# A Conformer block on one core: the passage from the convolution to the second feed-forward rearranged, and some of VectorE's work changed

## The chip, the core and the metric

The kernel runs on one core of a Trainium2 chip. The metric is the device time in microseconds of one execution. Lower is better. TensorE does matrix products into PSUM banks; VectorE (DVE), ScalarE (ACT) and GpSimd (POOL) do element-wise work; SyncE (SP) issues most DMAs. The kernel has eight PSUM banks of 128 x 512 float32: s0 to s3 and y0 to y3.

## What is computed

The input x has 2 sequences of 4000 tokens with 512 features. The reference, cut to what matters:

```python
h = _layernorm(x);  h = _silu(h @ w_ff1_a) @ w_ff1_b
x1 = x + 0.5 * h
h = _layernorm(x1); q, k, v = h @ w_q, h @ w_k, h @ w_v
p = _softmax(jnp.einsum('btd,bsd->bts', q, k) * scale)
x2 = x1 + jnp.einsum('bts,bsd->btd', p, v) @ w_o
h = _layernorm(x2) @ w_pw1
h = h[..., :D] * _sigmoid(h[..., D:])
dc = sum(pad(h)[:, i:i + T, :] * dw[i] for i in range(3))      # depthwise convolution over time
dc = (dc - mean) / sqrt(var + 1e-5)                            # per feature, over all tokens of both sequences
x3 = x2 + _silu(dc) @ w_pw2
h = _layernorm(x3); h = _silu(h @ w_ff2_a) @ w_ff2_b
return _layernorm(x3 + 0.5 * h)
```

The normalisation of `dc` runs over all tokens, so that nothing behind it can start before the depthwise convolution of the last token.

## The kernel before, in words

The 8000 tokens are cut into 16 chunks of 512 (`NCK`); the last chunk of each sequence has 416. A chunk has four tiles of 128 tokens, the features four blocks of 128 (`DC`, the index `cc` or `jj`). The stages follow each other: first feed-forward over all chunks; attention over all chunks `g`, 32 key tiles `kt` each; the convolution, whose chunk t runs beside attention of chunk t+1; the second feed-forward.

**The order of work.** The kernel's functions don't issue instructions. Each operation becomes a `Node` of a `Plan`, with reads, writes, an estimated duration and an engine that is fixed when it is written. `Plan.once` then goes through time and gives every engine, whenever it is free, the ready node that is due first; TensorE's blocks may overtake each other within 8 us, and other engines look ahead 16 us. `Plan.run` does six such passes, takes the shortest by its own costs and emits the instructions in that order. So the order of the program states the dependences, and the plan makes the queues. Since all instructions are emitted from one helper, the profile gives L93 for nearly every line; groups are told apart by tiles: `work` (LayerNorm and small tiles, normalised tokens, queries, z), `keys` (keys, feed-forward activations, the depthwise result dcv), `sums` (forms for attention), `wff` (feed-forward weights, and during the convolution its buffers), `xt` (tokens), `s` and `y` (PSUM).

**Attention.** Exponentials go to bf16 tiles. `pair_sums` forms sums for a product scheme with seven products in place of eight and adds the row sums of each group of two tile pairs to the float32 tile `acc`, one addition per pair. When a chunk is finished, `split_sums` writes `acc` as two bf16 parts, `sums_by_query` transposes both by DMA and reduces them on VectorE (`TENSOR_REDUCE`), and a reciprocal gives `rl`, which `project` needs for the residual x2. `sums_direct` does the same by matmuls with a column of ones; before the change only the fallback program uses it.

**The convolution.** `conv_b` does the gate half of `pw1` and its Sigmoid (Tanh for earlier chunks), `conv_a` the other half and the product into `G`, with `halo_left` and `halo_right` copying edge columns between chunks. For chunks 0 to 12, and block 0 of chunk 13, `taps_beside` does the depthwise step beside attention: ScalarE multiplies by the first tap into a float32 `tmp`, two `scalar_tensor_tensor` on VectorE add the others, `bn_stats` takes statistics. The rest of chunk 13 and chunks 14 and 15 are done by `depthwise` on TensorE: three matmuls with diagonal matrices `dwd`, then statistics and a copy to `dcv`. `conv_part` gathers the statistics of the chunks so far, `conv_scale` and `conv_shift` give scale and shift, `swish` does the Silu.

**The passage.** After attention (`attention_end`), `program` projects chunk 15, normalises its tiles (`ln_tiles`), and fills TensorE with `pw1` of chunk 14 and depthwise of chunk 13. After chunk 15's transposes (`transpose_pair`), each block of chunk 15 gets `conv_b`, `conv_a`, and `finish`: depthwise of chunk 15 and of chunk 14, then the scale. `pw2_x` puts the tokens into PSUM with an identity, `pw2` adds Silu times w_pw2, `ln_tiles` normalises chunk 0's four tiles out of PSUM, two `transpose_pair` follow, and the first block of the second feed-forward starts. Chunk 1's four tiles are done the same way in between, and all eight are copied from PSUM to `XT`. `ff2(c)` is the second feed-forward of chunk c; its `hook(f)` places, at block f of 16, the Silus and `pw2` of chunks ahead and the LayerNorm of the next chunk.

Of the kernel before, what the change touches and what calls it, by code (L numbers as in the profile page):

```python
# [15 lines left out]
TILE = 128  # L16
# [88 lines left out]
class Node:  # L105

    __slots__ = ("e", "emit", "dur", "land", "preds", "succs", "left", "ready", "late", "at", "seq", "ev", "size", "turn")


class Plan:  # L110
# [62 lines left out]
    def new(self, e, dur, land, emit, reads, writes, dkeys=()):  # L173
        n = Node()
        n.e, n.dur, n.land, n.emit, n.preds, n.succs, n.seq, n.at = e, dur, land, emit, set(), [], len(self.nodes), len(self.pe)
        n.size, n.turn = 0, False
        self.nodes.append(n)
        n.preds |= self.link(n, reads, writes, dkeys)
        return n

    def op(self, e, fn, reads, writes, inc):
# [21 lines left out]
        self.block = [] if inc else [n]  # L203

# [31 lines left out]
    def run(self):  # L236
# [17 lines left out]
        for n in best[1]:  # L254
            for f in n.emit:
                f()

    def once(self):
# [7 lines left out]
        for n in self.nodes:  # L266
            n.left, n.ready = len(n.preds), 0.0
            if not n.left:
                wait[n.e].append(n)
# [4 lines left out]
        def choose(e):  # L274
# [17 lines left out]
            for n in can:  # L292
                end = now + max(n.dur, n.size / 260) + self.OVER[e]
# [7 lines left out]
        while len(order) < len(self.nodes):  # L301
# [3 lines left out]
            s, n = min([c for c in said.values() if c], key=lambda c: c[0])  # L305
            wait[n.e].remove(n)
            ask[n.e] = True
            free[n.e] = s + n.dur + self.OVER[n.e]
            order.append(n)
# [11 lines left out]
            for u in n.succs:  # L321
# [3 lines left out]
                if not u.left:  # L325
                    wait[u.e].append(u)
                    ask[u.e] = True
# [3 lines left out]
class Sync:  # L331
# [110 lines left out]

    def dma(self, e, dkey, *fns, reads=(), writes=()):
# [82 lines left out]
class Conformer:  # L526
# [9 lines left out]
    KEEP = 1  # L536

# [20 lines left out]
    def memory(self):  # L558
# [164 lines left out]
        self.asb = [W.view(8192 + k * 2048, CHUNK, F32) for k in range(3)]  # L723
        self.b_asb = [W.buf("asb", 8192 + k * 2048, 4 * CHUNK) for k in range(3)]
        self.tmp = W.view(12288, CHUNK, F32)
        self.b_tmp = W.buf("tmp", 12288, 4 * CHUNK)
# [7 lines left out]
        self.th = [W.view(24576 + s * 2048, CHUNK, F32) for s in range(2)]  # L734
        self.b_th = [W.buf("th", 24576 + s * 2048, 4 * CHUNK) for s in range(2)]
# [4 lines left out]
        self.b_z = [[C.buf("z", o + cc * 2 * CHUNK, 2 * CHUNK) for cc in range(DC)] for o in (oM, oQ0)]  # L740
        assert off[0] == 47104
# [230 lines left out]
    def away(self, eng, dst, src, b_ps, writes):  # L972

        if eng == "ACT":
            self.act(dst, src, AF.Copy, [b_ps], writes)
        else:
            self.S.op("DVE", lambda e: e.tensor_copy(dst, src), reads=[b_ps], writes=writes)
# [63 lines left out]
    def ln_stats(self, c, sl, ti, src=None):  # L1041
        x, b_x = self.tokens(c, ti, src)
        self.S.op("DVE", lambda e: e.bn_stats(self.st[sl][:, ti, 0:6], x), reads=[b_x], writes=[self.b_st[sl][ti]])
# [15 lines left out]
    def ln_norm(self, c, sl, ti, out, b_out, eng, src=None):  # L1059
        x, b_x = self.tokens(c, ti, src)  # L1060
        if eng == "DVE":
            self.S.op("DVE", lambda e: e.tensor_scalar(
                out, x, self.mv[sl][:, ti, 0:1], self.rs[sl][:, ti:ti + 1],
                ALU.subtract, ALU.mult),
                reads=[b_x, self.b_mv[sl][ti], self.b_rs[sl][ti]], writes=[b_out])
# [657 lines left out]
    def pair_sums(self, g, j, step):  # L1723
# [337 lines left out]
    def units_late(self, o, kt):  # L2061
# [5 lines left out]
        elif kt < 7:  # L2067
# [3 lines left out]
            if kt == 2:  # L2071
                self.split_sums(o)
                self.sums_by_query(o % TCB % 2, 5)
# [22 lines left out]
    def attention_end(self):  # L2096
# [102 lines left out]
    def split_sums(self, g):  # L2199
# [9 lines left out]
        for hi, lo, acc in parts:  # L2209
            S.op("DVE", lambda e: e.tensor_copy(hi, acc), reads=[self.b_acc[s]], writes=[self.b_hl[0]])  # L2210
# [57 lines left out]
    def conv_b(self, t, jj):  # L2268
# [6 lines left out]
        else:  # L2275
            self.act(self.th[k][:, 0:W], ps[:, 0:W], AF.Sigmoid, [b_ps], [self.b_th[k]])

    def conv_a(self, t, jj):
# [4 lines left out]
        out = self.G[gs][:, jj, 1:1 + W]  # L2283
        wr = [self.b_G[gs][jj], self.b_Gl[gs][jj], self.b_Gr[gs][jj]]
        if t == NCK - 2 and jj >= self.KEEP:

            asb, b_asb = self.asb[jj % 3], self.b_asb[jj % 3]
            self.act(asb, ps[:, 0:CHUNK], AF.Copy, [b_ps], [b_asb], scale=2.0)

            def gate(eng):  # L2290
                self.S.op(eng, lambda e: e.tensor_tensor(out=out, in0=asb, in1=th, op=ALU.mult),
                          reads=[b_asb, self.b_th[k]], writes=wr)
# [4 lines left out]
        elif t == NCK - 1:  # L2297
            self.S.op("DVE", lambda e: e.scalar_tensor_tensor(
                out=out, in0=ps[:, 0:W], scalar=2.0, in1=th, op0=ALU.mult, op1=ALU.mult),
                reads=[b_ps, self.b_th[k]], writes=wr)  # L2300
# [4 lines left out]
        if t < NCK - 1:  # L2305
            self.halo_left(t, jj)
# [18 lines left out]
    def taps_beside(self, t, cc):  # L2325
# [5 lines left out]
        tmp, b_tmp = self.tmp[:, 0:W], self.b_tmp  # L2331
        self.act(tmp, g[:, 0:W], AF.Identity, rd, [b_tmp], scale=w[0])
        S.op("DVE", lambda e: e.scalar_tensor_tensor(
            out=tmp, in0=g[:, 1:1 + W], scalar=w[1], in1=tmp, op0=ALU.mult, op1=ALU.add),
            reads=rd + [b_tmp], writes=[b_tmp])

        def rest():
            dst, b_dst = (self.stage[cc], self.b_stage[cc]) if t < self.NBESIDE else (self.dcv[t][cc], self.b_dcv[t][cc])
            dst = dst[:, 0:W]
            S.op("DVE", lambda e: e.scalar_tensor_tensor(  # L2340
                out=dst, in0=g[:, 2:2 + W], scalar=w[2], in1=tmp, op0=ALU.mult, op1=ALU.add),
                reads=rd + [b_tmp], writes=[b_dst])
            S.op("DVE", lambda e: e.bn_stats(self.bst[:, cc, t, :], dst),
                 reads=[b_dst], writes=[self.b_bst[cc]])
            if t == self.beside(cc) - 1:
# [7 lines left out]
    def beside(self, cc):  # L2353
        return self.NBESIDE + (cc < self.KEEP)

# [547 lines left out]
```

## Time and profile before

| | us |
|---|---|
| median of three runs | 1888.24 (1886.43 to 1888.3) |
| the profiled execution | 1886.77 |
| its span, first to last instruction | 1882.5 |
| busy: TensorE, VectorE, ScalarE, GpSimd | 1859.6, 1570.6, 1180.4, 129.9 |
| granted TensorE clock | 1.0 |

Times in the profile count from the start of the span. The first feed-forward ends near 378, attention near 1400, and the second feed-forward begins at 1439.79. A row of a timeline gives start, duration, engine, line, operation, the tiles written and read, sizes and types, how many instructions are merged, and in brackets the engine's idle time before it and what ended it. A row of a group gives the count, then busy time and the mean in ns of one, then the idle time ahead of it by releaser. A matmul's duration includes its latency, so consecutive ones overlap.

### The profile page before, as it was taken

To read this page: it belongs to the slowest core of one execution; us is meant where nothing else is said; L and a number is where in the kernel's file an instruction comes from. 1 tells how busy PE (TensorE), PEld (TensorE's weight loads), DVE (VectorE), ACT (ScalarE), POOL (GpSimd) and SP (SyncE) were. 2 spreads that over 40 slices of the span, in tenths; PEclk is the share of its full clock that TensorE was granted. 3 is DMA by queue.
4 is the path that set the end of the run, shared out by engine and by line. 5 is a ranking of instruction groups with operands and counts; after the bars stand their busy time and mean duration, and the time that the engine had idled before them with its cause. 6 is when DMAs were issued, how large, how long until landed. Compare 5 with 4: busy or idle time off the path is not lost.

```text
span 1882.5 us, 38836 instructions
## 1 busy us (share of the span) xinstructions
PE 1859.6 (99%) x15362; PEld 1442.7 (77%) x15362; DVE 1570.6 (83%) x3315; ACT 1180.4 (63%) x2061; POOL 129.9 (7%) x235
## 2 busy tenths in 40 slices
PE   9999999999999999999999999999998999999998
PEld 5888888866777777777677777777764888888886
DVE  7888888868879888888888788889877888888875
ACT  5777777644555665565446555655557777777773
POOL 1000000000000000000000000000011000000000
PEclk9999999999999999999999999999999999999999
DMA  7323344197555665448944443444365222212111
GB/s 190 102 78 91 81 113 107 61 263 214 173 143 141 172 168 162 108 131 176 239 143 131 126 123 105 124 141 121 109 209 169 77 57 69 78 46 60 50 43 33
DMA packets 327186, 232.01 MB, mean 123 GB/s; under 512 B 206355, under 2 KB 297814, under 8 KB 326742
## 3 DMA queue, kind: packets, MB, share of 16 engines
q1 hardware_dynamic: 326470, 229.20, 44.3%
q8 instruction: 123, 2.02, 0.4%
q14 instruction: 65, 0.53, 0.1%
q10 hardware_dynamic: 528, 0.26, 0.0%
HBM read 128.44 MB, written 55.79 MB: 98 GB/s over the span
## 4 chain that ended last, share of the span: by engine, by line
PE 93%; DVE 3%; ACT 1%; DMA 1%; issue 0%; POOL 0%; SPq 0%; DVEq 0%; ACTq 0%
PE y L93 47%; PE s L93 47%; DVE work L93 1%; ACT work L93 1%; DVE xt L93 1%; DMA work<-work 1%; DVE s L93 0%; DVE sums L93 0%; DVE wff L93 0%; ACT sums L93 0%; DMA vhd<-wff 0%; DMA xt<-in_x_dram 0%; DMA wff<-keysd 0%; ACT xt L93 0%; ACT keys L93 0%
## 5 line engine op out<-in xcount | busy, mean ns | idle before, releaser
L93 ACT ACTIVATE sums<-s 128x512 bf16<-128x512 f32 (+2 forms) x494 | 289.0, 586 | 262.4 <-PE s L93 261.6
L93 ACT ACTIVATE keys<-s 128x512 bf16<-128x512 f32 (+1 forms) x281 | 165.0, 589 | 186.8 <-PE s L93 170.3
L93 PE MATMUL y<-work,keys 128*128 128x256 bf16 x1920 | 244.7, 273 | 0.0
L93 DVE TENSOR_TENSOR sums<-sums 128x512 bf16<-128x512 bf16 (+3 forms) x528 | 192.4, 396 | 46.8 <-ACT sums L93 44.1
L93 PE MATMUL s<-work,keys 128*128 128x256 bf16 (+5 forms) x1456 | 224.9, 292 | 0.0
L93 DVE BATCH_NORM_STATS2 work<-xt 128x6 f32<-128x512 bf16 x311 | 205.3, 682 | 7.6 <-DMA xt<-in_x_dram 5.6
L93 PE MATMUL y<-wff,keys 128*128 128x256 bf16 (+3 forms) x1592 | 209.0, 276 | 0.1
L93 PEld LDWEIGHTS y<-work,keys 128*128 128x128 bf16 x1920 | 187.9, 98 | 25.2
L93 PE MATMUL y<-sums,keys 128*128 128x256 bf16 (+1 forms) x1440 | 200.9, 270 | 0.0
L93 PE MATMUL s<-sums 128*128 128x256 bf16 x1296 | 194.0, 273 | 0.0
L93 DVE TENSOR_TENSOR keys<-keys 128x1024 bf16<-128x1024 bf16 (+2 forms) x262 | 168.7, 662 | 19.9 <-ACT keys L93 14.0
L93 PE MATMUL y<-work,wff 128*128 128x256 bf16 (+2 forms) x1116 | 184.0, 292 | 0.0
L93 PEld LDWEIGHTS y<-wff,keys 128*128 128x128 bf16 (+1 forms) x1592 | 151.1, 98 | 32.6 <-issue 3.3
L93 ACT ACTIVATE work<-xt,work 128x512 bf16<-128x512 bf16 x204 | 161.8, 808 | 10.2 <-DVE work L93 10.1
L93 POOL TENSOR_TENSOR work<-work 128x4 f32<-128x4 f32 (+2 forms) x94 | 89.4, 952 | 1107.3 <-DVE work L93 1089.1
L93 PEld LDWEIGHTS y<-sums,keys 128*128 128x128 bf16 x1440 | 139.1, 98 | 24.1 <-issue 0.4
L93 PEld LDWEIGHTS s<-work,keys 128*128 128x128 bf16 (+1 forms) x1456 | 118.7, 97 | 49.7 <-issue 3.7
L93 DVE TENSOR_TENSOR work<-work,sums 128x512 f32<-128x512 f32 (+1 forms) x224 | 150.5, 672 | 2.5
L93 PE MATMUL s<-work,wff 128*128 128x512 bf16 (+4 forms) x660 | 139.9, 347 | 2.9 <-DVE work L93 1.5
L93 PE MATMUL y<-sums,xt 128*128 128x256 bf16 (+1 forms) x960 | 141.9, 270 | 0.5 <-DVE sums L93 0.5
L93 PEld LDWEIGHTS s<-sums 128*128 128x128 bf16 x1296 | 126.7, 98 | 20.0
L93 PE MATMUL s<-work 128*128 128x512 bf16 (+1 forms) x541 | 135.6, 380 | 1.9 <-DVE work L93 1.2
(133 smaller groups left out, 3136.1 us busy)
## 6 DMA issues: line engine op xcount, KB each, us to landing
xt<-kfd SPq DMA_DIRECT2D x98, 384.0 KB, 3.2
xt<-v12d SPq DMA_DIRECT2D x105, 256.0 KB, 2.9
xd<-xt SPq DMA_DIRECT2D x28, 512.0 KB, 3.0
xt<-xd SPq DMA_DIRECT2D x28, 512.0 KB, 4.1
out_dram<-xt SPq DMA_DIRECT2D x14, 512.0 KB, 3.2
xt<-in_x_dram SPq DMA_DIRECT2D x13, 512.0 KB, 4.1
dcvd<-wff SPq DMA_DIRECT2D x48, 128.0 KB, 2.1
keys<-dcvd SPq DMA_DIRECT2D x12, 512.0 KB, 3.6
```

The costliest lines, as they stand in the source:

```text
L93: return getattr(eng, self.name)(*self.args, **self.kw)
```

## The change

1. **Planner.** `either` makes a node that may run on one of two engines; `once` gives it to whichever takes it first. Used for copies out of PSUM (`away`), the high part in `split_sums`, normalisations marked "any", and chunk 14's gates.
2. **Depthwise.** Chunk 14's four blocks come before chunk 15's `pw1`, each beside a block of chunk 13 and around the transposes. They cover 510 columns; chunk 15's cover 418, and its first two go to chunk 14 (`EDGE = 2`). Chunk 15's results use the ring of s banks.
3. **Sums.** Chunks 14 and 15 of attention use `sums_direct` (16 one-column matmuls in all) in place of DMA transposes and the reduction.
4. **Silus and first blocks in halves.** For chunks 0 and 1 each Silu is split in two halves of 256 columns. The first two blocks of the second feed-forward run on 256 columns, then on the other 256, into banks `heads`.
5. **Pairs.** Chunk 0's tiles are normalised two by two, each pair with its own factor and shift; the second pair's statistics wait for the first pair's results, some copies and Silus too (`behind`).
6. **Chunk 1.** Tiles 2 and 3 move into `ff2(0)`, at blocks 2 and 4, with a residual on VectorE in place of the identity. Chunk 2's Silus move to blocks 2, 3, 5, 6; the LayerNorm of chunk 1 moves to ScalarE, later blocks.
7. **Lighter VectorE.** `pair_sums` adds the two tiles of a group in bf16 into P30 and then once into `acc` (groups 1 to 6). `taps_beside` multiplies all three taps on ScalarE into bf16 and adds twice in bf16. `asb`, `tmp` and chunk 14's Sigmoids become bf16. `conv_part` gathers after chunk 9 (`PART = 10`) and writes on GpSimd.

```diff
+    def either(self, fns, reads, writes):
+        ...
+        n = self.new(ways[0][0], ways[0][1], ways[0][1], ways[0][2], reads, writes)
+        n.other = {e: (dur, emit) for e, dur, emit in ways}
...
         if j == 0:
             S.op("DVE", lambda e: e.tensor_copy(acc, sig[0]), reads=b_f[0:2], writes=[self.b_acc[s]])
-        elif step - 4 < n:
+        elif j == GROUPS - 1:
             S.op("DVE", lambda e: e.tensor_tensor(out=acc, in0=acc, in1=sig[step - 4], op=ALU.add),
                  reads=b_f[0:2] + [self.b_acc[s]], writes=[self.b_acc[s]])
+        else:
+            two = self.P30[:, 0:W].rearrange("p (h k) -> p h k", h=2)
+            out, x, y, rd, b_out = ((two, sig[0], sig[1], b_f[0:2], self.b_P30), (acc, acc, two, [self.b_P30, self.b_acc[s]], self.b_acc[s]))[step - 4]
+            S.op("DVE", lambda e: e.tensor_tensor(out=out, in0=x, in1=y, op=ALU.add), reads=rd, writes=[b_out])
...
-                self.sums_by_query(o % TCB % 2, 5)
+                if o < NCK - 2:
+                    self.sums_by_query(o % TCB % 2, 5)
+            if kt == 3 and o == NCK - 2:
+                self.sums_direct(o % TCB % 2)
...
-        self.sums_by_query(o % TCB % 2, 6)
         self.tick()
         self.late_third(o, 2, range(PAIRS))
+        self.sums_direct(o % TCB % 2)
...
-        self.act(tmp, g[:, 0:W], AF.Identity, rd, [b_tmp], scale=w[0])
-        S.op("DVE", lambda e: e.scalar_tensor_tensor(
-            out=tmp, in0=g[:, 1:1 + W], scalar=w[1], in1=tmp, op0=ALU.mult, op1=ALU.add),
-            reads=rd + [b_tmp], writes=[b_tmp])
+        for k, (x, b_x) in enumerate(homes):
+            self.act(x, g[:, k:k + W], AF.Identity, rd, [b_x], scale=w[k])
+        def add(to):
+            (x, b_x), (y, b_y) = homes[0], homes[to]
+            S.op("DVE", lambda e: e.tensor_tensor(out=y, in0=x, in1=y, op=ALU.add), reads=[b_x, b_y], writes=[b_y])
...
-        drains = [self.depthwise(tail - 1, self.KEEP)]
-        for k in range(2):
-            self.transpose_pair(k, 1, ("ACT", "DVE")[k], ybank(), last)
-        drains.append(self.depthwise(tail - 1, DC - 2))
+        dw(tail, 0, ybank())
+        for k in range(2):
+            dw(tail - 1, k + 1, ybank())
+            copy_away()
+            self.transpose_pair(k, 1, ("ACT", "DVE")[k], ybank(), last)
+            dw(tail, k + 1, ybank())
+            copy_away()
+            if k == 0:
+                gate("DVE")
+        dw(tail - 1, DC - 1, ybank())
+        copy_away()
+        dw(tail, DC - 1, ybank())
+        copy_away()
...
-        for cc in range(DC):
-            self.swish(1, cc)
-        self.pw2_x(0, all_t[2:], banks[2:])
-        self.pw2(0, all_t, banks, False)
+        for k in range(0, TPC, 2):
+            self.pw2(0, all_t[k:k + 2], banks[k:k + 2], False)
...
+        heads = [self.sbank() for _ in all_t]
+        for cc in range(DC):
+            self.swish(1, cc, 0)
+        self.pw2_x(1, (0, 1), heads[2:])
+        self.pw2(1, (0, 1), heads[2:], False)
+        self.early = heads[0:2]
+        for k in range(2):
+            pair = (2 * k, 2 * k + 1)
+            for ti in pair:
+                self.ln_stats(0, sl, ti, x, ((), (), self.b_mv[sl][0:2], self.b_sh[sl][0:2])[ti])
+            ...
+            for ti in pair:
+                self.ln_norm(0, sl, ti, self.ltm[ti][0:TILE, :], self.b_ltm[ti], "any", x)
+                self.transpose_pe(ti, 0, "ACT", heads[ti])
+        for h in range(2):
+            for f, (ps, b_ps) in enumerate(self.early):
+                out = ps[:, h * HC:(h + 1) * HC].rearrange("p (t k) -> p t k", t=2)
+                for cc in range(DC):
+                    self.mm(out, self.Wa[:, cc, f * 128:(f + 1) * 128], self.lnT[0][:, 2 * h:2 * h + 2, cc, 0:TILE],
+                            cc == 0, cc == DC - 1, [self.b_Wa[f * self.NWA // FC]] + self.b_lnT[0][2 * h:2 * h + 2], b_ps)
...
-                if c == 0 and f < 4:
-                    self.swish(n, f)
+                if c == 0 and f == 0:
+                    for cc in range(DC):
+                        self.swish(1, cc, 1, behind=self.b_lnT[0][0:1])
+                if c == 0 and f in (2, 4):
+                    ti = 1 + f // 2
+                    bank = [self.sbank()]
+                    self.pw2(1, [ti], bank)
+                    self.after(1, lambda: self.pw2_residual(1, [ti], bank))
+                if c == 0 and f in (2, 3, 5, 6):
+                    self.swish(n, (2, 3, 5, 6).index(f), behind=self.b_lnT[0][2:4])
...
-                        self.ln_job(1, "in", "DVE", (1, 1, 2, 2, 3, 4, 5, 6, 7, 8))
+                        self.ln_job(1, "in", "ACT", (3, 4, 5, 7, 7, 8, 8, 8, 9, 9))
```

More of the change, by code (lines that the diff above doesn't have):

```diff
@@ L268, in once @@
             if not n.left:
-                wait[n.e].append(n)
+                for e in n.other or (n.e,):
+                    wait[e].append(n)
         head, done, starts = 0, [False] * len(pe), [0.0] * len(pe)
@@ L325, in once @@
                 if not u.left:
[L326 to L327 removed]
+                    for o in u.other or (u.e,):
+                        wait[o].append(u)
+                        ask[o] = True
         return free["PE"], order, starts
@@ L536 @@
     KEEP = 1
+    PART = 10
+    EDGE = 2
     CONV_SLOTS = 3
@@ L2705, in program, with dw @@
         gate("DVE")
-        drains = [self.depthwise(tail - 1, self.KEEP)]
-        for k in range(2):
-            self.transpose_pair(k, 1, ("ACT", "DVE")[k], ybank(), last)
-        drains.append(self.depthwise(tail - 1, DC - 2))
-        gate("DVE")
-        self.load(self.Wp2, i["w_pw2"].rearrange("(c p) f -> p c f", p=128), [self.b_Wp2])
-        for f, copy in drains:
-            f()
-            copy()
-        copies = []
-        def finish(cc, between=None):
-            for t in (last, tail):
-                f, copy = self.depthwise(t, cc)
-                f()
-                copies.append(copy)
-                if t == last and between:
-                    between()
-            self.conv_scale(cc)
+        copies = []
+        def dw(t, cc, bank):
+            copies.append(self.depthwise(t, cc, bank))
         def copy_away(eng="ACT"):
```

259 lines of the change are left out of this document (142 added, 117 removed).

## The prediction

> **What bounds the kernel now.** I read the page's busy times first, then busy time by stage (windows of the span), then TensorE's timeline with the idle time before each group.
>
> ```profile
> span 1882.5 us, 38836 instructions
> PE 1859.6 (99%) x15362; PEld 1442.7 (77%) x15362; DVE 1570.6 (83%) x3315; ACT 1180.4 (63%) x2061; POOL 129.9 (7%) x235
> ```
>
> TensorE is busy 1859.6 of 1882.5 us: whatever the change does to the other engines, it can win 22.9 us of TensorE's idle time plus any matmuls that it drops. The windows (columns: length, then busy time of PE, PEld, DVE, ACT, POOL) say where that idle time lies.
>
> ```profile
> 378.00:1370.00 992.00, 986.33 (x7941) 727.66 (x7940) 833.37 (x1778) 548.98 (x970) 53.22 (x125) 1.00 0.56 154
> 1370.00:1400.00 30.00, 26.87 (x280) 22.49 (x278) 22.86 (x56) 17.60 (x34) 1.67 (x5) 1.00 0.64 186
> 1400.00:1415.20 15.20, 12.24 (x69) 5.48 (x67) 12.09 (x26) 7.09 (x11) 5.54 (x17) 1.00 0.67 208
> 1415.20:1440.00 24.80, 21.47 (x113) 10.01 (x114) 16.70 (x39) 19.12 (x32) 5.12 (x12) 1.00 0.64 199
> 1440.00:1458.00 18.00, 18.00 (x89) 8.59 (x88) 16.08 (x32) 13.62 (x23) 1.02 (x1) 1.00 0.50 165
> 1458.00:1862.00 404.00, 404.00 (x3478) 340.09 (x3477) 334.66 (x682) 294.72 (x510) 28.13 (x28) 1.00 0.21 57
> ```
>
> TensorE idles 5.67 us in attention (378 to 1370), 3.13 at its end, 2.96 between 1400 and 1415.2, 3.33 from there to the second feed-forward, and nothing after that until the last chunk. What the change touches thus holds 15.1 us. The gaps of the passage, by releaser:
>
> ```profile
> 1410.84 0.40 PE L93 MATMUL y<-work 128*128 128x128 bf16 x4 [0.42 <-ACT work L93]
> 1411.64 0.40 PE L93 MATMUL y<-work 128*128 128x128 bf16 x4 [0.40 <-DVE work L93]
> 1412.94 0.81 PE L93 MATMUL y<-wff 128*128 128x512 bf16 x3 [0.91 <-POOL wff L93]
> 1415.21 2.97 PE L93 MATMUL s<-work,wff 128*128 128x416 bf16 x16 [1.24 <-ACT keys L93]
> 1429.67 1.04 PE L93 MATMUL s<-work 128*128 128x512 bf16 x4 [0.30 <-ACT work L93]
> 1431.08 1.04 PE L93 MATMUL s<-work 128*128 128x512 bf16 x4 [0.37 <-ACT work L93]
> 1435.27 0.40 PE L93 MATMUL y<-work 128*128 128x128 bf16 x4 [0.78 <-ACT work L93]
> 1437.90 0.40 PE L93 MATMUL y<-work 128*128 128x128 bf16 x4 [0.25 <-DVE work L93]
> 1439.79 6.20 PE L93 MATMUL s<-work,wff 128*128 128x512 bf16 x28 [1.49 <-DVE work L93]
> ```
>
> The first four wait for chunk 15's normalised tiles, their transposes and copies, the next two for Silus, the last three for chunk 0's LayerNorm.
>
> **The change part by part.**
>
> *Depthwise of chunk 14 sooner; sums by matmul.* Chunk 15's LayerNorm starts with residuals that need the softmax sums:
>
> ```profile
> 1402.71 1.22 DVE L93 TENSOR_REDUCE work<-work 128x4 f32<-128x1024 bf16 x1 [1.31 <-DMA work<-work]
> ...
> 1404.23 1.41 DVE L93 SCALAR_TENSOR_TENSOR xt<-s,work,xt 128x512 bf16<-128x512 f32 x2
> ```
>
> ```profile
> 1400.70 1.90 PE L93 MATMUL s<-work,wff 128*128 128x512 bf16 x8
> 1408.73 1.46 PE L93 MATMUL y<-wff 128*128 128x512 bf16 x6
> 1410.03 0.39 PE L93 MATMUL y<-work 128*128 128x128 bf16 x4
> ```
>
> The transposing DMAs, their wait and the 1.22 us reduction go, so the first residual can follow its projection, which TensorE could issue from 1400.7 instead of the fill that stands there: some 1.5 us sooner. And four depthwise groups of chunk 14 (12 matmuls; the six from 1408.73 give way to the next group at 1410.03, so 0.217 each: 2.6 us) now come while TensorE waits for chunk 15. Gap and fill match: of 2.96 us I leave 0.4, **-2.6**; at worst nothing goes, because each group first needs its gate on VectorE or GpSimd. The two extra columns (EDGE) let chunk 14 run without chunk 15's first column; they cost four small copies on ScalarE or VectorE, hidden there. On SP the load of w_pw2 moves behind these groups; its first use is behind the Silus, so it has some 10 us to spare.
>
> *Silus and first blocks in halves, tiles in pairs.* Chunk 15's groups lose the fill that moved ahead (8 + 3 instead of 8 + 6 matmuls per channel) and their four PSUM banks now also hold the depthwise results, whose statistics and copy follow each other: room for a new wait of about 0.5. Behind them the Silus begin; a half has 256 columns, and the nearest rows have 512 and 416:
>
> ```profile
> L93 ACT ACTIVATE work<-keys,work 128x512 bf16<-128x512 bf16 x56 | 43.4, 809 | 8.1 <-PE y L93 7.8 <-PE s L93 0.3
> L93 ACT ACTIVATE work<-keys,work 128x416 bf16<-128x416 bf16 x8 | 5.7, 731 | 1.7 <-PE y L93 1.7
> ```
>
> ```profile
> 1423.71 1.28 ACT L93 ACT_TABLE_LOAD   x1
> 1425.01 0.20 ACT L93 ACTIVATE work<-work 128x1 f32<-128x1 f32 x1
> 1428.11 6.44 ACT L93 ACTIVATE work<-keys,work 128x512 bf16<-128x512 bf16 x9
> 1434.44 0.77 ACT L93 ACTIVATE work<-s,work 128x512 bf16<-128x512 f32 x1
> ```
>
> ```profile
> L93 POOL TENSOR_TENSOR work<-work 128x1 f32<-128x1 f32 x18 | 10.7, 597 | 26.8 <-DVE work L93 26.6
> L93 ACT ACTIVATE work<-y 128x512 bf16<-128x512 bf16 x5 | 3.0, 595 | 5.4 <-PE y L93 5.3
> L93 DVE BATCH_NORM_STATS2 work<-s 128x6 f32<-128x512 f32 x4 | 2.6, 672 | 3.0 <-PE s L93 3.0
> ```
>
> 96 columns cost 0.078 us, so a half is an estimated 0.60, or 0.51 where nine whole ones take 0.715 each. The last Silu before the first products shortens by 0.2, the eight split ones cost ScalarE 8 x 0.3 = 2.4 us more in all, with chunk 2's four no longer in between. Then the pair: statistics of two tiles instead of four, so the first transposes start about 1.3 us sooner, and the first two blocks run on half a chunk while the other pair is normalised. Against that TensorE's fill shrinks: two tiles of chunk 1 (eight matmuls and two identities, 2.1 us) move into the second feed-forward. The chain behind the first pair's products is two statistics (1.3), factor (0.6), shift (0.15), normalisation (0.8), transposes (0.4), copy (0.6), and six hand-overs that I estimate at 0.15 each: 4.7 us, in which TensorE has 12 matmuls of 0.217 and 0.8 of transposes. So I leave 1.5 idle there, and 0.5 at the banks: 3.33 becomes 2.0, **-1.3**, between -3.3 and +1. The new waits (the second pair's statistics wait for the first pair's shift, chunk 1's copies too) queue on VectorE and ScalarE only work that is due later; the weight loads on SP stay issued in the order of before.
>
> [...]
>
> *Lighter VectorE.* In attention's row sums, two float32 additions per group become one of bf16 and one of float32, in 6 groups of 16 chunks; a depthwise step beside attention turns two scalar_tensor_tensors into two bf16 additions and one ScalarE multiplication into three, 52 times.
>
> ```profile
> L93 DVE TENSOR_TENSOR work<-work,sums 128x512 f32<-128x512 f32 x196 | 134.1, 684 | 2.0
> L93 DVE TENSOR_TENSOR sums<-sums 128x512 bf16<-128x512 bf16 x408 | 157.5, 419 | 42.1 <-ACT sums L93 39.9
> L93 DVE SCALAR_TENSOR_TENSOR wff<-wff,work 128x512 f32<-128x512 bf16 x49 | 36.4, 744 | 0.5 <-ACT wff L93 0.5
> L93 DVE SCALAR_TENSOR_TENSOR wff<-wff,work 128x512 bf16<-128x512 bf16 x48 | 35.8, 746 | 0.8
> L93 ACT ACTIVATE wff<-wff,work 128x512 f32<-128x512 bf16 x49 | 35.3, 720 | 12.3 <-POOL wff L93 11.3 <-DVE wff L93 0.7
> ```
>
> ```profile
> PE s L93 <- DVE s L93: 2.8, 7, 0.8
> PE s L93 <- DVE xt L93: 2.4, 3, 1.1
> ACT sums L93 <- PE s L93: 256.3, 262, 3.3
> ```
>
> VectorE saves 96 x 0.265 = 25 us and 52 x 0.65 = 34 us: its 84% of attention falls to 78%. ScalarE gains 52 x 1.44 = 75 us: 55% becomes 63%. The waits of attention's window alone (last three rows: total, times, longest) show that TensorE waits there for VectorE, 5.2 us of the 5.67, and hardly for ScalarE. But the long ones (1.0 to 1.1) stand behind a VectorE reduction that itself waits for a transposing DMA, as at 1402.71, and 14 chunks keep that. I take **-0.8** for attention (bounds -5.7 and, by the rival below, +10.4) and **-1.2** of the 3.13 at its end, where chunk 15's shorter columns make VectorE's fixed costs weigh most and chunk 14's reduction also goes. Reusing P30 as scratch makes one bf16 addition per chunk wait for the previous chunk's last product; its neighbours have whole steps of slack. The partial statistics go to GpSimd (7% busy): nobody waits for them until the final scale, whose aggregate grows by under 0.1.
>
> *TensorE's own work.* Two identities go (0.43). Two direct sums add 16 one-column matmuls, each behind a 128-column weight load. Nearest row: the four 128-column transposes from 1410.03 in 0.39, so 0.1 each, or by
>
> ```profile
> L93 PE MATMUL y<-work 128*128 128x128 bf16 x64 | 6.0, 220 | 2.8 <-DVE work L93 1.6 <-ACT work L93 1.2
> ```
>
> at 0.22 for one, 0.06 for each further one: 1.0 to 1.6, I take 1.0. Net **+0.55**.
>
> *The second feed-forward's chunk 0.* It receives four half Silus (2.0), chunk 2's Silus (2.9), four normalisations moved from VectorE (2.9) and up to four copies (2.0): 9.8 us of ScalarE. Cover: 4.4 us that ScalarE idles between 1440 and 1458, 1.7 of matmuls that come with it, and later chunks, where it is 73% busy. Uncovered: 0 to 3.7; I take **+0.5**.
>
> The engine that the planner may now choose for copies and normalisations I cost at 0 (±0.5): it moves no work on TensorE.
>
> Sum: -2.6 - 1.3 - 0.8 - 1.2 + 0.55 + 0.5 = -4.85. The profiled execution took 1886.77 (4.27 around its span), so 1881.9; the runs' median, 1888.24, lies 1.47 above it. In its terms: **1883.4 us**. A measurement of this kernel can tell about 0.2%, 3.8 us, from no change.
>
> **The rivals.**
>
> *Larger gain (0.18).* VectorE's relief ends nearly all waits of attention: -4.5 and -2.0 in place of -0.8 and -1.2, sum -9.35, 1878.9. For it: nearly every wait there names VectorE. Against: the DMA behind the longest ones stays.
>
> *It returns (0.13).* The planner orders by its own costs, so "sooner" in the program need not be sooner on TensorE; and the fill taken from chunk 1 is missed. Then the passage's -1.3 is 0 and chunk 0 pays 3.7: sum -0.35, 1887.9. For it: ScalarE is already 76% busy from 1440 to 1458. Against: the Silus for chunk 3 can wait for the next chunk.
>
> *Slower (0.16).* Three ScalarE multiplications in a row stand ahead of an exponential that frees the bank of the next scores. Each trio is 1.44 us longer; if TensorE waits 0.2 of that 52 times, +10.4 replaces -0.8: sum +6.35, 1894.6. Slower than before from 0.08 us per trio, by more than 0.2% from 0.15. For it: scores, ScalarE's copies, VectorE's sums and exponentials form one ring over three banks. Against: ScalarE waits for TensorE, 256 us in 262 places for the exponentials alone, far more than the reverse.
>
> [...]
>
> **How the numbers follow.** Forecast 0.53 (sum -2 to -7.8, 1880 to 1886; 0.33 of it beyond 0.2%). Faster: 0.33 + 0.18 = 0.51. Slower: 0.16, and 0.02 of the returning case. Same: 0.31. The range, 1877 to 1891, takes in the larger gain and the slow side to +2.8 us; about 0.06 lies below it and 0.10 above.
>
> **What would show it.** Right: matmuls of the depthwise weights between the transposes near 1410 with under 0.5 us idle; no reduction ahead of chunk 15's residuals; first blocks of 256 columns some 3 us sooner behind the last gate; VectorE near 78% in attention. Wrong: TensorE waiting for ScalarE in attention, idle time after the first blocks, or the gap near 1415 unchanged because gates come late.

## The result and the profile after

The changed kernel takes 1879.56 us (median of 6 runs, 1878.1 to 1880.57), the kernel before beside it 1887.83 (6 runs, 1886.43 to 1888.3): a ratio of 0.9953, 95% interval 0.9943 to 0.9964. That is 8.3 us less; 4.85 was forecast. The profiled execution took 1879.47; that of before, 1886.77, lies 1.1 below its median, so the two profiles show 7.3 of the 8.3.

The busy times of the page, changed kernel:

```profile
span 1875.6 us, 38994 instructions
PE 1857.5 (99%) x15384; PEld 1445.4 (77%) x15384; DVE 1548.0 (83%) x3293; ACT 1278.0 (68%) x2190; POOL 124.2 (7%) x241
```

The span is 6.9 shorter. TensorE idles 18.1 us in place of 22.9; ScalarE is busy 98 us longer and VectorE only 23 less. (A busy total depends on the order too: the changed kernel's operations in another order, e8 below, have VectorE at 1517.9, which is 53 less.) The windows, same columns as before:

```profile
378.00:1370.00 992.00, 989.28 (x8001) 733.37 (x8000) 797.02 (x1771) 626.36 (x1094) 49.57 (x139) 1.00 0.56 155
1370.00:1400.00 30.00, 28.51 (x270) 21.40 (x268) 19.96 (x44) 17.56 (x35) 1.42 (x7) 1.00 0.59 178
1400.00:1415.20 15.20, 12.92 (x67) 6.08 (x67) 12.82 (x27) 6.64 (x11) 4.47 (x15) 0.89 0.35 99
1415.20:1440.00 24.80, 21.85 (x123) 10.78 (x121) 21.20 (x50) 21.44 (x40) 4.69 (x7) 1.00 0.77 236
1440.00:1458.00 18.00, 18.00 (x124) 11.85 (x123) 15.79 (x31) 15.53 (x27) 1.77 (x2) 1.00 0.39 116
1458.00:1862.00 404.00, 403.86 (x3456) 337.74 (x3454) 348.65 (x682) 306.13 (x508) 29.45 (x28) 1.00 0.21 57
```

Work shifts across window edges when attention gets shorter, so a landmark is safer. The last product of attention is such a one; the first fence is the timeline of before, the second that of after:

```profile
1400.42 0.35 PE L93 MATMUL y<-wff,sums 32*128 32x208 bf16 x2
```

```profile
1394.30 0.35 PE L93 MATMUL y<-wff,sums 32*128 32x208 bf16 x2
```

Up to there the change wins **6.1 us**. The forecast had 1.0: 0.8 and 1.2, less 1.0 for the direct sums, which all stand ahead of this landmark. No work moved behind it: 11545 matmuls start before it in place of 11525, and 16 of the 20 more are the direct sums. From there to the end of the span, 482.1 before and 481.3 after, it wins **0.8**, where 3.85 was forecast. So the total came out inside the forecast's range, and the place did not fit it. The gaps of the passage, timeline of TensorE after:

```profile
1405.67 0.40 PE L93 MATMUL y<-work 128*128 128x128 bf16 x4 [0.97 <-ACT work L93]
1406.98 0.82 PE L93 MATMUL y<-wff 128*128 128x510 bf16 x3 [0.91 <-DVE work L93]
...
1408.89 2.61 PE L93 MATMUL y<-wff 128*128 128x512 bf16 x6 [0.39 <-ACT keys L93]
1411.34 3.68 PE L93 MATMUL s<-work,wff 128*128 128x416 bf16 x20
...
1421.79 0.61 PE L93 MATMUL y<-work 128*128 128x512 bf16 x2 [0.80 <-ACT work L93]
...
1427.12 0.40 PE L93 MATMUL s<-work 128*128 128x128 bf16 x4 [0.41 <-ACT work L93]
1427.79 0.40 PE L93 MATMUL s<-work 128*128 128x128 bf16 x4 [0.27 <-ACT work L93]
1428.96 0.60 PE L93 MATMUL s<-work,wff 128*128 128x256 bf16 x4 [0.78 <-ACT work L93]
1430.08 0.62 PE L93 MATMUL s<-work 128*128 128x128 bf16 x8 [0.52 <-DVE work L93]
1431.31 3.62 PE L93 MATMUL s<-work,wff 128*128 128x256 bf16 x20 [0.17 <-DVE work L93]
```

The gap of 1.24 ahead of chunk 15's first block is gone, but 0.97 and 0.91 stand between the transposes, and the six 512-column matmuls from 1408.89 take 2.61 us where six took 1.46 before: TensorE runs there at half clock (below).

In attention TensorE's waits shrink. Views of waits, window 378 to 1390 (total, times, longest), TensorE's and VectorE's, before and then after:

```profile
PE s L93 <- DVE s L93: 4.2, 10, 0.8
PE s L93 <- DVE xt L93: 2.4, 3, 1.1
...
DVE work L93 <- DMA work<-work: 6.7, 7, 2.0
```

```profile
PE s L93 <- DVE s L93: 1.4, 4, 0.4
PE s L93 <- ACT sums L93: 1.3, 3, 0.6
PE s L93 <- DVE xt L93: 0.6, 2, 0.4
...
DVE work L93 <- DMA work<-work: 2.2, 3, 0.9
```

The last row is the surprise: VectorE's waits for the transposing DMAs, which the forecast took to stay in 14 chunks, fall from 6.7 to 2.2 us, though 14 of the 16 reductions are still there. What moved them?

### The profile page after: what moved, and what is told of

Read it like the earlier page. It is cut to its first block, busy times and chain, and to the rows that moved or that the text cites. A ratio compares the mean times of both kernels' runs of the same rounds, so it can differ in the third digit from the quotient of the medians.

```text
span 1875.6 us, 38994 instructions
## 1 busy us (share of the span) xinstructions
PE 1857.5 (99%) x15384; PEld 1445.4 (77%) x15384; DVE 1548.0 (83%) x3293; ACT 1278.0 (68%) x2190; POOL 124.2 (7%) x241
## 4 chain that ended last, share of the span: by engine, by line
PE 97%; DVE 1%; ACT 1%; DMA 0%; issue 0%; SPq 0%; DVEq 0%; ACTq 0%
PE s L93 49%; PE y L93 49%; DVE work L93 1%; ACT work L93 0%; DVE wff L93 0%; DMA xt<-in_x_dram 0%; ACT sums L93 0%; DVE xt L93 0%; DVE s L93 0%; ACT xt L93 0%; ACT s L93 0%; DVE sums L93 0%; DVE keys L93 0%; ACT keys L93 0%; SPq L93 0%
## 5 line engine op out<-in xcount | busy, mean ns | idle before, releaser
L93 ACT ACTIVATE keys<-s 128x512 bf16<-128x512 f32 (+2 forms) x284 | 165.2, 587 | 141.4 <-PE s L93 115.8
L93 DVE TENSOR_TENSOR sums<-sums 128x512 bf16<-128x512 bf16 (+3 forms) x528 | 201.8, 399 | 63.5 <-ACT sums L93 53.1
L93 PE MATMUL y<-sums,keys 128*128 128x256 bf16 (+1 forms) x1440 | 204.8, 270 | 0.0
L93 POOL TENSOR_TENSOR work<-work 128x4 f32<-128x4 f32 (+3 forms) x92 | 88.3, 963 | 1108.3 <-DVE work L93 1108.3
L93 PE MATMUL s<-work,wff 128*128 128x512 bf16 (+5 forms) x668 | 140.5, 345 | 1.4 <-ACT work L93 1.1
L93 PE MATMUL s<-work 128*128 128x512 bf16 (+4 forms) x565 | 137.5, 373 | 2.4 <-DVE work L93 1.7
L93 PEld LDWEIGHTS y<-work,wff 128*128 128x128 bf16 x1116 | 108.2, 98 | 29.7
```

What stands on the lines that cost most here:

```text
L93: return getattr(eng, self.name)(*self.args, **self.kw)
```

## The experiments

**Single parts.** Four kernels in one series, e1 to e4: before with the group sums in bf16 alone,

```diff
...
+            two = self.P30[:, 0:W].rearrange("p (h k) -> p h k", h=2)
+            out, x, y, rd, b_out = ((two, sig[0], sig[1], b_f[0:2], self.b_P30), (acc, acc, two, [self.b_P30, self.b_acc[s]], self.b_acc[s]))[step - 4]
...
```

before with the taps alone,

```diff
-        self.act(tmp, g[:, 0:W], AF.Identity, rd, [b_tmp], scale=w[0])
+        for k, (x, b_x) in enumerate(homes):
+            self.act(x, g[:, k:k + W], AF.Identity, rd, [b_x], scale=w[k])
...
```

before with all of the attention side (both of these, the direct sums of the last two chunks, the smaller edits beside them), and the reverse, the changed kernel with the group sums and the taps undone. The direct sums are in both of the last two.

> The kernel before with one part of the change: two tiles of a group are added in bf16 and then once into the float32 row sums. Theory VectorE's queue: attention became shorter because TensorE's waits for VectorE went, and this part is 25 of the 59 us that VectorE saves there: about -2.5 us. Rival, direct sums and order: the lighter additions are hidden anyway, and attention's gain comes from the direct sums and a new order: 0, within 0.7 us.

> The kernel before with one part of the change: three multiplications on ScalarE and two bf16 additions in place of one multiplication and two scalar_tensor_tensors. VectorE's queue: 34 of 59 us, about -3.5 us. Rival, ScalarE pays: the 75 us more on ScalarE delay exponentials, +1 to +10 us. Rival, direct sums and order: 0, within 0.7 us.

> The kernel before with all that the change does beside and inside attention (row sums, taps, partial statistics earlier and on GpSimd, direct sums for chunks 14 and 15, choice of engine for the high part), and the passage as before. VectorE's queue: all of attention's 6 us, so -6 to -7. By the split that the prediction gave: -0.8 - 1.2 + 1.0, so -1, and -2.5 if the direct sums also bring chunk 15's residuals forward. If attention's gain depends on the new passage: 0 to -2.

> The changed kernel with the row sums and the taps as before. VectorE's queue: the gain left is that of the direct sums and the passage, -1 to -2.5 us against the kernel before. By the prediction's split: -2.85 (-4.85 without the -0.8 and -1.2). Direct sums and order: most of the -8.3 stays, -6 or more.

| | ratio to before (95%) | span | attention's last product |
|---|---|---|---|
| before | 1 | 1882.5 | 1400.42 |
| e1, group sums alone | 0.9989 (0.9980 to 0.9998) | 1882.2 | 1399.39 |
| e2, taps alone | 0.9992 (0.9983 to 1.0001) | 1883.6 | 1400.48 |
| e3, attention's side | 0.9979 (0.9970 to 0.9988) | 1882.6 | 1399.03 |
| e4, passage's side | 0.9986 (0.9977 to 0.9995) | 1881.9 | 1400.38 |
| the change | 0.9953 (0.9943 to 0.9964) | 1875.6 | 1394.30 |

By the medians e1 is 1.7 us below before, e2 1.7, e3 4.1 and e4 2.6. Only e4 lands on the split that the prediction gave (2.85); e1 and e3 fall between their theories.

The rival of ScalarE's trios falls: in e2 three multiplications on ScalarE cost nothing that the interval (0.9983 to 1.0001) shows, and TensorE's waits for ScalarE in attention are 1.3 us in e2 as in before. But the parts don't add up: attention's side alone ends attention 1.4 us sooner, the whole change, with the same operations there, 6.1. The passage cannot make attention shorter by its operations; it can by the planner. `Plan.run` makes six passes and emits the order of the one that ends first by its own costs, the passage included. Its modelled ends put before, and attention's side, on the fifth pass, the passage's side on the second and the change on the first; the six lie within 4 us. So an edit of the passage exchanged the order of all of attention. (The group sums alone took the third pass, the taps alone the second, so e1 and e2 differ from before in their order too.)

**The pass held fixed.** For three kernels `PASSES` is 1, for the last the fifth pass is taken:

```diff
-    PASSES = 6
+    PASSES = 1
```

```diff
-            if best is None or end < best[0]:
+            if turn == 4:
```

> The kernel before, emitted in the order of the planner's first pass instead of its fifth (by the planner's own costs the first ends 1.98 us later: 1859.25 against 1857.27). Nothing else differs. Theory 'the pass' (which pass's order attention gets is worth several us on the chip, beyond what the planner's costs say): some us of difference, in either direction, with the steps between chunks of attention changed. Theory 'the parts' (attention's gain comes from its operations and the passage together): within 1 us of the kernel before, +2 at most, as the planner says.

> The attention side of the change (e3) in the order of the planner's first pass, the pass that the changed kernel takes; e3 took the fifth. Theory 'the pass': attention's last product starts 5 to 6 us sooner than before (near 1395) as in the changed kernel, and the time is 3 to 5 us below e3's, some 1880 to 1882. Theory 'the parts': as e3, attention 1 to 2 us shorter than before and the time 1884 to 1886.

> The passage's side of the change (e4) in the order of the planner's first pass; e4 took the second. Theory 'the pass': attention differs from e4's by over 1 us in either direction, with the same operations. Theory 'the parts': attention ends within 0.5 us of before, the time as e4, 1886 to 1887. In both the passage itself gives 1 to 2.5 us as in e4.

> The changed kernel, all parts, in the order of the planner's fifth pass in place of the first (by its own costs 0.65 us later). Theory 'the pass': attention loses 3 to 5 of its 6.1 us and the time is 1882 to 1885. Theory 'the parts': attention keeps 5 to 6 us and the time is 1879.5 to 1880.5.

| ratio; attention's last product; from there to the end | fifth pass | first pass |
|---|---|---|
| before | 1; 1400.42; 482.1 | e5: 0.9989 (0.9980 to 0.9998); 1399.02; 484.4 |
| attention's side | e3: 0.9979; 1399.03; 483.6 | e6: 0.9952 (0.9938 to 0.9965); 1394.55; 481.9 |
| passage's side | not run | e7: 0.9965 (0.9953 to 0.9977); 1397.18; 481.2 |
| the whole change | e8: 0.9972 (0.9961 to 0.9982); 1397.45; 481.4 | 0.9953 (0.9943 to 0.9964); 1394.30; 481.3 |

"The pass" holds: e6 gets all that the change gets, without its passage, and the change at the fifth pass loses 3.15 us of attention. But the order does it only together with the lighter work on VectorE. Against before, attention's last product comes 1.4 us sooner with the first pass alone (e5), 1.4 sooner with attention's side alone (e3), and 5.9 sooner with both (e6).

Read down the fifth pass's column, the change is worth 5.1 us (medians 1889.01 and 1883.89), of which 3.0 in attention; the other 3 us of its 8.3 come with the first pass. Read down the first pass's column, each side alone wins most of what both win over e5, and the passage adds nothing to attention's side that the intervals show: 0.9953 against 0.9952. The times behind attention are not of one kind: in these profiles TensorE runs at half clock in the passage for some 6.8 us in e5, for 3.4 in e3, e6, e7 and the change, and not at all in before and e8 (mean granted clock from the end of attention's last product to 1440: 0.92, 0.96 and 1.00). Two cautions. With other operations the same pass is not the same queue, so a column separates operations from order only to an us or two. And the interval of e8's ratio touches that of the change.

**What the order does.** In all the kernels VectorE's waits for the transposing DMAs (`work<-work`) and TensorE's waits for VectorE's `xt` tiles rise and fall together, roughly. Totals in us, window 378 to 1390:

| | VectorE for the DMA | TensorE for VectorE's xt |
|---|---|---|
| group sums alone (third pass) | 10.0 | 3.8 |
| change, fifth pass | 7.9 | 2.4 |
| attention's side, fifth pass | 7.4 | 2.1 |
| before (fifth pass) | 6.7 | 2.4 |
| taps alone; passage's side (second pass) | 5.8; 5.2 | 1.6; 1.6 |
| first pass: passage's side; before; change; attention's side | 3.0; 2.5; 2.2; 2.1 | 0.6 each |

They don't order the kernels by their time: the group sums alone wait most and still end attention 1.0 us sooner than before. The first try to move these waits was one number of the planner, in before and in the change at the fifth pass:

```diff
-            self.transpose(self.sT[:, h], self.hl[:, h].rearrange("p c k -> p (c k)"), [self.b_hl[h]], [self.b_sT[h]])
+            node = self.transpose(self.sT[:, h], self.hl[:, h].rearrange("p c k -> p (c k)"), [self.b_hl[h]], [self.b_sT[h]])
+            if S.plan:
+                node.land += 1000
```

> The kernel before, at the fifth pass that it took, with one number of the planner changed: the DMAs that transpose the softmax sums are taken to land 1 us later, so that VectorE's reductions behind them are placed later. Same instructions. Theory 'VectorE held by the DMA': the waits of VectorE for those DMAs in attention (6.7 us in 7 places before) fall below 3, attention's last product starts 1 to 3 us sooner than before's 1400.42, and the time is 1 to 3 us below before. Rival 'any other order is as good': the waits fall but attention ends within 0.7 us of before, in either direction.

> As the previous one on the changed kernel at its fifth pass (e8, 7.9 us in 10 such waits, attention's last product at 1397.45). Theory 'VectorE held by the DMA': waits below 3 us, the product 1.5 to 3 us sooner, near 1395, and the time 1.5 to 3 us below e8's ratio of 0.9972, so about 0.996. Rival: within 0.7 us of e8, ratio 0.997.

It missed: the waits were 8.1 and 8.6 us, not below 3, so neither theory was tested. The ratios were 1.0014 (1.0005 to 1.0023) and 0.9973 (0.9963 to 0.9984), attention's last product at 1402.88 and 1398.41. The waits of TensorE for `xt` were 3.3 and 3.2. The edit doesn't do what it was meant to: `once` sets `n.land = pipe - s + 1000` anew when it places a DMA, so the added 1 us is gone before a reduction is placed, and only the due times of the first of the six passes feel it. In before the fifth pass comes out as another order on every engine. In the change it comes out as e8's order, operation by operation, so e11 is a repeat of e8. That is worth having: the ratio repeats (0.9972 and 0.9973), but the two profiles of one order differ by 1.0 us in attention's last product and by 0.7 and 0.8 us in the two waits.

The second try moved the reductions by hand, after planning:

```diff
...
+        order = best[1]
+        for m in self.push:
+            i = next(k for k, (n, e) in enumerate(order) if n is m)
+            j, passed = i, 0
+            while passed < 4 and order[j + 1][0] not in m.succs:
+                j += 1
+                passed += order[j][1] == "DVE"
+            order.insert(j, order.pop(i))
...
```

> The changed kernel at its fifth pass (e8), with one thing done after planning: each reduction of transposed softmax sums, and the reciprocal behind it, is queued on VectorE behind up to four further operations (as far as no operation passed needs it). Same instructions, everything else in e8's order. In e10 and e11 the changed estimate left those waits in place (8.1 and 8.6 us), so they did not test this. Theory 'VectorE held by the DMA': its waits for the transposing DMAs, 7.9 us in 10 places in e8, three of them 1.4 to 1.9 long, fall below 2.5, TensorE's waits for VectorE behind them go, attention's last product starts 1.4 to 3 us before e8's 1397.45, and the ratio goes from 0.9972 to about 0.996. Rival 'the order elsewhere': the waits fall and attention still ends within 0.7 us of e8's, ratio 0.997.

VectorE's timeline around one reduction, first the change at the fifth pass, then with the reduction pushed back:

```profile
1217.90 1.22 DVE L93 TENSOR_REDUCE work<-work 128x4 f32<-128x1024 bf16 x1 [1.88 <-DMA work<-work]
1219.04 0.68 DVE L93 BATCH_NORM_STATS2 wff<-wff 128x6 f32<-128x512 bf16 x1
```

```profile
1216.58 0.69 DVE L93 BATCH_NORM_STATS2 wff<-wff 128x6 f32<-128x512 bf16 x1
1218.19 1.22 DVE L93 TENSOR_REDUCE work<-work 128x4 f32<-128x1024 bf16 x1 [0.92 <-DMA work<-work]
```

The statistics that stood behind the reduction now run while the DMA is under way. The waits of that kernel, same view as above:

```profile
PE s L93 <- DVE xt L93: 0.6, 2, 0.3
...
DVE work L93 <- DMA work<-work: 2.9, 3, 1.1
```

The link is shown: with 5.0 us less waiting for the DMA than in e8 (5.7 less than in its repeat), TensorE's waits for `xt` fall from 2.4 (3.2) to 0.6. What it is worth is less sure. Attention's last product comes at 1396.68, 0.8 us sooner than in e8, where 1.4 to 3 were expected, and 1.7 sooner than in the repeat; counted from the last product of the first chunk it is 1.2 and 1.7. The ratio, 0.9959 (0.9946 to 0.9973), overlaps e8's. So an estimate for the DMA waits is 1 to 1.7 us of the 3 to 4 that the pass is worth in attention, with 0.5 to 1 us between two profiles of one order. Of the rest, TensorE's waits for VectorE's `s` tiles are some (3.4 in this kernel, 1.4 in the change); which feature of the order ends them stays open.

**The half clock.** Windows of 1 us of the changed kernel (busy times as above, then the granted clock):

```profile
1404.00:1405.00 1.00, 0.70 (x4) 0.10 (x1) 1.00 (x2) 0.20 (x1) 0.75 (x1) 1.00 1.09 404
1405.00:1406.00 1.00, 0.33 (x4) 0.23 (x4) 0.97 (x4) 0.62 (x1) 0.46 (x1) 1.00 0.62 248
1406.00:1407.00 1.00, 0.09 (x3) 0.02 (x2) 1.00 (x3) 0.60 (x1) 1.00 (x6) 1.00 0.00 0
1407.00:1408.00 1.00, 1.00 (x9) 0.64 (x10) 1.00 (x3) 0.00 (x0) 0.14 (x2) 0.92 0.00 0
1408.00:1409.00 1.00, 0.61 (x6) 0.34 (x5) 1.00 (x3) 0.75 (x2) 0.00 (x0) 0.50 0.00 0
...
1411.00:1412.00 1.00, 1.00 (x6) 0.54 (x5) 1.00 (x3) 0.60 (x1) 0.00 (x0) 0.87 0.00 0
```

After three us with TensorE busy 0.70, 0.33 and 0.09, and most of one in which it is busy throughout, the clock falls to 0.50 for about 3.4 us. The gaps of 0.97 and 0.91 lie ahead of the fall, that of 0.39 behind it. To see whether the gaps do it, eight matmuls without use fill the gap of 0.97, put in after planning:

```diff
+                if c == NCK - 1 and k == 0 and n == 1 and cc == 0 and self.S.plan:
+                    for _ in range(8):
+                        self.S.plan.block[-1].emit.insert(0, lambda: self.S.emit_op("PE", lambda e: e.matmul(
+                            ps[:, 256:512], self.ident, self.Wp1[:, 0, 0:256], start=True, stop=True),
+                            [self.b_ident, self.b_Wp1], [b_ps], False))
```

> The changed kernel in its own order, with eight idle matmuls of 256 columns (their result is overwritten) placed after planning ahead of the second group of chunk 15's transposes, where TensorE idles 0.97 us in the changed kernel. Nothing else differs. Theory 'the close gaps halve the clock': the granted clock stays at 1.00 between 1407 and 1412 and the six depthwise matmuls that took 2.61 us take 1.5; what follows comes 1 to 1.5 us sooner, and the time is 1 to 1.5 us below the changed kernel's, a ratio to before of about 0.9945. Rival 'the clock falls for another reason (the transposes themselves, or the two later gaps of 0.91 and 0.39)': it falls to 0.50 all the same, and the time is the changed kernel's or up to 0.3 longer. Third possibility: the clock stays, but the Silus or LayerNorm chains take the time back, ratio 0.9953 as before.

Timeline of TensorE with the gap filled:

```profile
1404.57 1.04 PE L997 MATMUL y<-wff,work 128*128 128x256 bf16 x8
...
1407.01 0.82 PE L93 MATMUL y<-wff 128*128 128x510 bf16 x3 [0.91 <-DVE work L93]
...
1409.15 1.24 PE L93 MATMUL y<-wff 128*128 128x512 bf16 x5 [0.88 <-ACT keys L93]
1410.24 3.68 PE L93 MATMUL s<-work,wff 128*128 128x416 bf16 x20
...
1430.20 3.62 PE L93 MATMUL s<-work,wff 128*128 128x256 bf16 x20 [0.17 <-DVE work L93]
...
1749.20 1.04 PE L93 MATMUL y<-work 128*128 128x512 bf16 x4 [0.59 <-DVE xt L93]
```

(The record of one of the six matmuls near 1409.15 is missing from this trace, so the gap of 0.88 is nearer 0.66.) The clock stays at 1.00, and chunk 15's first blocks start at 1410.24 in place of 1411.34, 1.1 us sooner, as expected. At 1430.20 the gain is still 1.1; then TensorE waits 0.59 us for VectorE in the second feed-forward, where the changed kernel has no such wait, and behind that 0.24 is left. The span is 1875.0, 0.6 shorter. The ratio is 0.9949 (0.9936 to 0.9963): the lowest of all the kernels, but not to be told from the change's 0.9953. So the expected gain in time is not shown. And this is one profiled execution of each kernel: equal gaps act in one place and not in another (last section), so it supports that the gaps halve the clock, and doesn't prove it.

## Why the prediction was right in its range and wrong in its parts

The time, 1879.56, lies inside 1877 to 1891, but the gain of 8.3 is 1.7 times the 4.85 of the sum: attention gave 5.1 us more than its terms and the passage some 3 less. That these errors went opposite ways is luck.

**Attention, -0.8, and its end, -1.2: the failed step.** It read rightly that TensorE waits there for VectorE behind reductions that wait for a DMA, and then said "14 chunks keep that". The order of before was taken as given; only the choice of engines was costed, at 0 (±0.5), not that the planner could change to another pass. At the fifth pass the waits do stay (7.9 us, 8.6 in the repeat) and attention gives 3.0 (2.0); at the first they go. Measured: -6.1. The rows of waits account for 4.3 of it (TensorE's waits from 378 to 1390 sum to 8.2 us before and 3.9 after). For the rest, TensorE's busy time up to the landmark also falls, from 1389.7 to 1388.0 us, with 20 matmuls more; so some stalls seem to count as busy, and idle time is no firm bound on what can be won.

**The larger gain (0.18)** gave 1878.9 and was the nearest of all cases: attention did change by what it said. VectorE's relief alone didn't do that (e3, 1.4 us); what spoke against it, the waits for the DMA, went with the new order.

**Depthwise of chunk 14 sooner, -2.6.** At the fifth pass it came as forecast; the gaps up to chunk 15's first blocks are 0.25 and 0.30 there (timeline of e8):

```profile
1408.54 1.74 PE L93 MATMUL y<-wff 128*128 128x512 bf16 x6 [0.25 <-ACT keys L93]
...
1412.56 3.68 PE L93 MATMUL s<-work,wff 128*128 128x416 bf16 x20 [0.30 <-DVE work L93]
```

In the order that the change has they are 0.97, 0.91 and 0.39 in place of 0.42, 0.40, 0.91 and 1.24, so -0.7, and the half clock takes 1.1 back. The sign that the prediction named, under 0.5 us idle between the transposes, fails there. The timeline of VectorE, changed kernel, says what the fill leaves behind:

```profile
1401.71 0.70 DVE L93 BATCH_NORM_STATS2 wff<-y 128x6 f32<-128x510 f32 x1 [0.22 <-PE y L93]
...
1405.64 0.70 DVE L93 BATCH_NORM_STATS2 wff<-y 128x6 f32<-128x512 f32 x1
1406.25 0.67 DVE L93 COPY work<-y 128x1024 bf16<-128x1024 bf16 x1
1406.84 0.76 DVE L93 TENSOR_SCALAR work<-xt,work 128x512 bf16<-128x512 bf16 x2
```

Every depthwise group that TensorE does sooner leaves statistics for VectorE in the same stretch, 0.7 each, and they stand between the steps of chunk 15's LayerNorm that TensorE waits for; VectorE is busy 0.97 to 1.00 in each us from 1404 to 1409. The forecast counted the gates ahead of the fill, and not the statistics behind it. They are not the whole cause: in e8 VectorE has the same statistics and is as busy (0.97 to 1.00 in each us from 1404 to 1413), and TensorE hardly waits. What in the order makes the difference was not tested.

**Halves and pairs, -1.3.** The six gaps sum to 2.95; before, five summed to 3.19: -0.2, inside its bounds (-3.3 to +1), but at the fifth pass they are 4.33, +1.1. The Silus were sized well. Timeline of ScalarE, changed kernel:

```profile
1417.40 1.28 ACT L93 ACT_TABLE_LOAD   x1
1418.69 0.20 ACT L93 ACTIVATE work<-work 128x1 f32<-128x1 f32 x1
...
1420.18 0.59 ACT L93 ACTIVATE work<-keys,work 128x256 bf16<-128x256 bf16 x1
1421.13 4.53 ACT L93 ACTIVATE work<-keys,work 128x256 bf16<-128x256 bf16 x9 [0.36 <-DVE work L93]
```

A half takes 0.59 alone and 0.50 in a row (0.60 and 0.51 forecast); the table switch again costs 1.28 with the next activation right behind it. What the pairs win in time they lose in fill: 2.95 us idle is left where the forecast left 1.5 + 0.5. A hand-over, taken at 0.15 there, is 0.06 in before from ScalarE's normalisation (1434.44, 0.77 long) to the transposes at 1435.27, and 0.15 from VectorE's copy (1438.96, 0.68 long) to the products at 1439.79. Which step of the chain takes the 0.95 more was not measured.

**TensorE's own work, +0.55**, came out lower, since eight one-column matmuls take 0.34 us, so 0.7 at most in place of 1.0. **Chunk 0 of the second feed-forward, +0.5:** the cover held; TensorE is busy 18.00 of 18.00 and 403.86 of 404.

**VectorE near 78% in attention:** 80%. ScalarE's 63% is right. **The slower rival (0.16)** was wrong in its mechanism: e2 has the trios, and its ratio is 0.9992 (0.9983 to 1.0001).

## What to carry to other kernels

Where a planner chooses among several orders whose modelled ends lie close together, a small edit in one place can redraw the queues everywhere: predict the edit at a fixed order, give the redraw a term of its own with both signs, and compare kernels with the order pinned before crediting a part. Compare the emitted orders as well: e11 was meant as a test and was the same order again. In such a kernel look for long waits for a DMA in the queue of the busiest helper engine, since what is queued behind them is late too, as the statistics are that start at 1219.04 in e8 and at 1216.58 in e12; and before moving fill into a gap, count what the fill leaves for the engine whose chain the gap waits for.

## What the runs showed of the hardware

Gaps of TensorE far shorter than the low stretch that follows can go before a fall of its clock: behind 0.97 and 0.91 us in some 3 us the changed kernel ran 3.4 us at 0.50, and with one of them filled it stayed at 1.00. It isn't their sum alone: before has 0.42, 0.40, 0.91 and 1.24 in 5 us at full clock. The clearest pair is the change at the fifth pass and the same with the reductions pushed back. Their windows of 3 us hold the same 13 matmuls with the same gaps (1.28 and 0.73); the second fence is the second kernel, and the second line of each is the 3 us that follow:

```profile
1428.00:1431.00 3.00, 1.10 (x13) 0.91 (x14) 2.93 (x10) 2.68 (x5) 0.49 (x2) 1.00 1.01 315
1431.00:1434.00 3.00, 1.24 (x15) 0.82 (x13) 2.11 (x8) 2.52 (x6) 0.26 (x1) 1.00 1.09 385
```

```profile
1427.20:1430.20 3.00, 1.09 (x13) 0.90 (x14) 2.93 (x10) 2.66 (x5) 0.50 (x2) 1.00 0.85 241
1430.20:1433.20 3.00, 2.01 (x14) 1.17 (x11) 1.80 (x7) 2.43 (x5) 0.27 (x1) 0.50 1.06 353
```

In the second kernel the clock is low from 1430.2 to 1437.0, some 6.8 us. Nor do executions of one program agree: of the 33 of before that were timed beside e1, the four with a mean granted clock of 0.997 have spans of 1885.3 to 1886.9 us, the one at 1.0 has 1882.7. The longest gap just ahead of the fall was 1.28 us in the second kernel and 0.97 in the changed kernel. What decides whether gaps act was not shown. At the 1.1 us by which chunk 15's first blocks came sooner in e9, a fall is as much as most of the terms of the forecast.
